# Token layout p\*16+i with whole transfers, full-array transforms, a second product path and a new instruction order in an S4-plus-gated-MLP kernel

## The chip, the cores and the metric

The kernel runs on 1 core of one Trainium2 chip. The metric is the device time of one execution in microseconds (us), lower is better. A profile gives the span from the first to the last instruction, which is about 2 us shorter than that time (276.0 of 278.0 us before). Engines are PE (TensorE, matmuls), DVE (VectorE), ACT (ScalarE), POOL (GpSimd) and SP (which only issues transfers here). Each has its own list of instructions, in the order in which the program emits them; semaphores join the lists. PSUM is the memory that PE writes its results to here, in banks; the other tiles are in SBUF.

## The reference, cut to what matters

```python
x  = A_u                                  # (1, 2048 tokens, 512)
xn = layernorm(x)
# branch A: S4 convolution. A kernel K (512 x 2048) is made from 128 complex modes,
#   K = real(einsum("dn,dnl,dn->dl", C, exp(dt*A*l), dt*B)),
# then y = irfft(rfft(xn, 4096) * rfft(K, 4096))[:2048] + xn * Dskip
# branch B: gated MLP, F = 1792
h  = sigmoid(xn @ w_gate) * (xn @ w_up)
out = x + A(xn) + h @ w_down
```

## The kernel before

Everything is a plan: each operation is added with its engine and dependencies, and a literal list `ORDER` of operation numbers says in which order they are emitted. The per-engine program is that list, filtered by engine. So `ORDER` decides, for each engine, what stands in front of what.

```python
ORDER = [1, 29, 0, 3, 2, 39, 12, 14, ... ]       # 930 numbers, found off-line
...
    def run(self):
        for n in ORDER or range(len(self.ops)):
            op = self.ops[n]
            for s in op.acq:                      # takes a buffer (a PSUM bank, an SBUF slot)
                s.idx = self.free[s.pool].pop(0)
            for s in op.rel:
                self.free[s.pool].append(s.idx)
            yield op
```

The gated part, four groups of 512 tokens with 14 slices each. There are only three PSUM banks ("gu") for gate and up results:

```python
def fg(...):                                       # gate: 4 matmuls 128x128x512
    T.matmul(bank(sl)[:, c0:c1], w[:, kt, k * 128:(k + 1) * 128], xnT[:, grp, kt, c0:c1], ...)
S.activation(out=hT_sb[...], in_=bank(a), func=ACT.Sigmoid)            # ACT frees the gate bank
def fu(...):                                       # up: 4 matmuls
    T.matmul(bank(sl), wu_sb[:, kt, k * 128:(k + 1) * 128], xnT[:, grp, kt, :], ...)
def fpd(sl=b, h=h):                                # DVE reads the up result out of PSUM
    V.tensor_tensor(out=h(), in0=h(), in1=bank(sl), op=ALU.mult)
prods.append(pl.add("DVE", 0.60, fpd, [es_, mu], PPROD, rel=[b]))      # and frees its bank
```

The convolution: a first transform (matrix S1), four blocks of correlation matmuls that build K from tables which DVE multiplies up (`cmul`), and for each of 16 units a second transform, products with the transform of K, an inverse transform, a trip through DRAM (`z_scr`, `v_scr`), and a last transform (S2).

```python
xv = A_u[0].rearrange("(a j i) d -> j a i d", j=2, i=NT)     # token a*32+j*16+i on partition 64*j+a
# load, store and sum: two transfers of 64 partitions each
for j in range(2):                                           # first transform: two half arrays
    T.matmul(bank(sl, j), s1[64 * j:64 * j + 64, :], xn[64 * j:64 * j + 64, i, :], ...)
for j in range(2):                                           # last transform: two half arrays
    T.matmul(o[64 * j:64 * j + 64, DW * p:DW * p + DW], s2[:], vps[p][t][:, j, r, :], ...)
```

## Time and profile before

| | before |
|---|---|
| time, median | 275.44 us (275.18 to 279.31, 4 runs) |
| span of the profiled run | 276.0 us (this execution took 278.01 us, more than the median) |
| mean granted clock (TensorE, 1 is full speed), same run | 0.965 |
| busy PE, DVE, ACT, same run | 229.2, 208.6, 162.7 us |

No engine is full over the whole run, so stages have to be looked at. I cut the trace at five events: the first gated matmul, the ends of the first, second and last block of correlation matmuls, and the end of the last inverse transform. The windows view of the kernel before, columns named in the first line here (busy us of each engine, number of instructions in brackets, granted clock, DMA share, GB/s):

```profile
core 0: us, PE busy (x) PEld busy (x) DVE busy (x) ACT busy (x) POOL busy (x), PEclk, DMA share, GB/s
0.00:15.17 15.17, 8.32 (x38) 4.27 (x39) 7.66 (x23) 5.01 (x9) 4.25 (x14) 0.86 0.72 190
15.17:94.60 79.43, 70.39 (x438) 31.51 (x437) 74.59 (x152) 72.01 (x117) 8.15 (x14) 0.96 0.59 158
94.60:121.20 26.60, 24.47 (x303) 12.08 (x302) 25.86 (x58) 13.13 (x23) 1.98 (x4) 1.00 0.55 146
121.20:195.70 74.50, 59.22 (x865) 33.48 (x865) 66.73 (x125) 41.37 (x62) 3.17 (x7) 0.98 0.49 136
195.70:242.80 47.10, 40.77 (x471) 23.33 (x471) 17.77 (x24) 28.36 (x35) 3.27 (x4) 0.96 0.70 184
242.80:276.00 33.20, 26.04 (x180) 12.96 (x179) 15.97 (x28) 2.81 (x4) 0.00 (x0) 0.97 0.55 162
```

Up to 195.7 us DVE is nearly full: in the second to fourth row it is busy 74.59 + 25.86 + 66.73 = 167.2 of 180.5 us. Behind that point PE has the most work. The gated products in the groups view (busy us, mean ns of one, idle before):

```profile
L964 DVE TENSOR_TENSOR hT_sb<-hT_sb,bank 128x512 bf16<-128x512 bf16 x56 | 37.0, 682 | 10.7 <-PE bank L957 6.0 <-ACT hT_sb L951 3.7 <-ACT ln_m_f L467 0.8
```

A product is recorded with 0.682 us and holds DVE 0.60 us when products follow one another (two of them take DVE from 35.46 to 36.66 us). Three lines of the chain of waits (start, us, what) show the start: the transposes wait for the identity matrix, and the first gated matmuls follow at 15.4 us.

```profile
4.63 7.99 DMA ident<-c_ident
12.66 1.87 PE pair L522 x16
...
15.38 12.50 PE bank L942 x64
```

### The profile page before, as it was taken

What the parts mean: (1) busy time and instruction counts of PE and PEld (TensorE: products, weight loads), DVE (VectorE), ACT (ScalarE), POOL (GpSimd) and SP (SyncE); (2) the same over time, 40 slices, a digit from 0 to 9 for tenths busy, and PEclk for the clock granted to TensorE, in tenths of its full rate; (3) what the DMA queues carried; (4) which work ended last, traced back from release to release, by engine and by line L of the source; (5) the groups of instructions that cost most, each with busy time, mean ns of one, the idle gap of its engine ahead of it and who ended that gap; (6) DMA issues with size and microseconds to landing.
All of it is one profiled execution on the core that took longest, in us unless ns stands there. A gap on an engine that the chain in (4) does not pass through costs nothing.

```text
span 276.0 us, 5805 instructions
## 1 busy us (share of the span) xinstructions
PE 229.2 (83%) x2290; PEld 117.6 (43%) x2290; DVE 208.6 (76%) x407; ACT 162.7 (59%) x249; POOL 20.8 (8%) x43
## 2 busy tenths in 40 slices
PE   7299997969969899878598878596998689799792
PEld 2264433323323544355354445243665345444441
DVE  3579899998999999999979997979153222685172
ACT  2289999998998572558385549341356758531000
POOL 3225000020020002003000000000011200000000
PEclk9779999997999999999999999989999979999998
DMA  5899992122066764451765751454386984665743
GB/s 152 190 297 306 201 307 77 40 57 76 31 190 160 233 160 128 100 183 28 184 185 143 222 159 46 130 153 125 93 221 178 223 199 112 190 187 181 217 134 97
DMA packets 51069, 43.42 MB, mean 157 GB/s; under 512 B 13153, under 2 KB 44258, under 8 KB 51042
## 3 DMA queue, kind: packets, MB, share of 16 engines
q1 hardware_dynamic: 47506, 38.73, 50.1%
q0 software_dynamic: 960, 1.57, 3.9%
q10 hardware_dynamic: 2576, 2.75, 3.5%
q8 instruction: 18, 0.29, 0.5%
q14 instruction: 9, 0.07, 0.1%
HBM read 24.43 MB, written 12.06 MB: 132 GB/s over the span
## 4 chain that ended last, share of the span: by engine, by line
PE 40%; DVE 29%; DMA 16%; ACT 6%; issue 4%; SPq 2%; DVEq 0%; ACTq 0%
PE bank L942 11%; PE bank L957 9%; DMA big<-z_scr 8%; PE bank L982 6%; DVE big L681 5%; DVE big L680 5%; PE pair L744 4%; DVE hT_sb L964 4%; PE pair L835 4%; DVE big L685 4%; DVE big L686 3%; DMA ident<-c_ident 3%; DMA big<-big 2%; DMA big<-v_scr 2%; SPq L397 2%
## 5 line engine op out<-in xcount | busy, mean ns | idle before, releaser
L942 PE MATMUL bank<-xnT,wg_sb 128*128 128x512 bf16 (+1 forms) x236 | 57.4, 382 | 1.4 <-ACT hT_sb L951 1.4
L957 PE MATMUL bank<-xnT,wu_sb 128*128 128x512 bf16 x224 | 55.9, 384 | 2.9 <-ACT hT_sb L951 1.5
L982 PE MATMUL bank<-wd_sb,hT_sb 128*128 128x512 bf16 x224 | 52.2, 387 | 3.3 <-ACT glu_sb L1012 3.3
L964 DVE TENSOR_TENSOR hT_sb<-hT_sb,bank 128x512 bf16<-128x512 bf16 x56 | 37.0, 682 | 10.7 <-PE bank L957 6.0
L951 ACT ACTIVATE hT_sb<-bank 128x512 bf16<-128x512 f32 x56 | 32.3, 599 | 15.1 <-PE bank L942 15.0
L841 DVE TENSOR_TENSOR big<-big 128x2048 bf16<-128x2048 bf16 x16 | 19.6, 1223 | 24.8 <-DMA big<-big 8.2
L680 DVE TENSOR_TENSOR big<-big 128x256 bf16<-128x256 bf16 (+5 forms) x52 | 33.1, 636 | 2.5 <-ACT big L721 1.4
L942 PEld LDWEIGHTS <-wg_sb 128*128 128x128 bf16 x236 | 22.8, 101 | 27.9 <-issue 6.8
L982 PEld LDWEIGHTS <-hT_sb 128*128 128x128 bf16 x224 | 21.7, 99 | 30.4 <-issue 6.9
L681 DVE TENSOR_TENSOR big<-big 128x256 bf16<-128x256 bf16 (+5 forms) x52 | 32.9, 633 | 0.0
L957 PEld LDWEIGHTS <-wu_sb 128*128 128x128 bf16 x224 | 20.5, 98 | 28.5 <-issue 7.7
L822 ACT ACTIVATE big<-pair 128x1024 bf16<-128x1024 f32 x16 | 16.3, 1026 | 11.4 <-PE pair L817 7.3
L685 DVE TENSOR_TENSOR big<-big 128x128 bf16<-128x128 bf16 (+5 forms) x52 | 21.9, 420 | 0.8
L835 PE MATMUL pair<-big 128*128 128x256 bf16 x160 | 20.4, 278 | 2.2 <-ACT big L837 0.7
L862 ACT ACTIVATE big<-pair 128x1024 bf16<-128x1024 f32 x16 | 16.4, 1026 | 9.0 <-PE pair L858 5.2
L686 DVE TENSOR_TENSOR big<-big 128x128 bf16<-128x128 bf16 (+5 forms) x52 | 21.6, 416 | 0.0
L837 ACT ACTIVATE big<-pair 128x1024 bf16<-128x1024 f32 x16 | 16.4, 1027 | 7.8 <-PE pair L835 3.4
L835 PEld LDWEIGHTS <-big 128*128 128x128 bf16 x160 | 15.9, 100 | 8.2 <-issue 3.0
L744 PE MATMUL pair<-big 128*32 128x82 bf16 x512 | 11.5, 257 | 8.2 <-DVE big L685 6.3
L645 ACT ACTIVATE big<-pair 128x1024 bf16<-128x1024 f32 x16 | 16.3, 1019 | 1.7 <-DMA z_scr<-big 1.0
L858 PE MATMUL pair<-big 64*64 64x256 bf16 x384 | 13.7, 272 | 3.1 <-ACT big L822 1.6
L817 PE MATMUL pair<-big,m 64*64 64x256 bf16 x128 | 6.6, 288 | 10.2 <-DMA big<-z_scr 10.2
(84 smaller groups left out, 234.2 us busy)
## 6 DMA issues: line engine op xcount, KB each, us to landing
big<-c_E SPq DMA_DIRECT2D x16, 320.0 KB, 4.2
z_scr<-big SPq DMA_DIRECT2D x16, 256.0 KB, 2.6
big<-z_scr SPq DMA_DIRECT2D x16, 256.0 KB, 4.6
big<-big SPq DMA_DIRECT2D x64, 64.0 KB, 2.9
v_scr<-big SPq DMA_DIRECT2D x16, 256.0 KB, 2.6
big<-v_scr SPq DMA_DIRECT2D x12, 256.0 KB, 4.6
big<-in_A_u_dram SPq DMA_DIRECT2D x8, 256.0 KB, 7.2
wu_sb<-in_B_w_up_dram SPq DMA_DIRECT2D x2, 896.0 KB, 6.1
```

What stands on the lines that cost most here:

```text
L680: V.tensor_tensor(out=wide(outp), in0=lov, in1=mre, op=ALU.mult)
L681: V.tensor_tensor(out=wide(tb()), in0=lov, in1=mim, op=ALU.mult)
L685: V.tensor_tensor(out=outp[:, :, :, 0, :], in0=outp[:, :, :, 0, :], in1=tb()[:, :, :, 1, :], op=opr)
L686: V.tensor_tensor(out=outp[:, :, :, 1, :], in0=outp[:, :, :, 1, :], in1=tb()[:, :, :, 0, :], op=opi)
L744: T.matmul(pk[32 * t:32 * t + 32, y % 4, :], G[:, r, :, comp, h], H[:, r, :, comp, h], start=(comp == 0), stop=(comp == 1), tile_position= ...
L835: T.matmul(two(sk)[:, o:o + DW], es()[:, g, kt, :], kT[p][:, kt, :], start=kt in (0, NKT - 1), stop=kt >= NKT - 2)
L841: V.tensor_tensor(out=pp().rearrange("p q h m -> p (q h) m"), in0=xx().rearrange("p q h m -> p (q h) m"), in1=kb()[:, 0:2 * DW].unsqueeze( ...
L942: T.matmul(bank(sl)[:, c0:c1], w[:, kt, k * 128:(k + 1) * 128], xnT[:, grp, kt, c0:c1], start=(kt == 0), stop=(kt == KT - 1))
L951: S.activation(out=hT_sb[:, hs.idx, k % 2, :], in_=bank(sl), func=ACT.Sigmoid)
L957: T.matmul(bank(sl), wu_sb[:, kt, k * 128:(k + 1) * 128], xnT[:, grp, kt, :], start=(kt == 0), stop=(kt == KT - 1))
L964: V.tensor_tensor(out=h(), in0=h(), in1=bank(sl), op=ALU.mult)
L982: T.matmul(bank(po), hT_sb[:, hts[k // 2].idx, k % 2, jj * 128:(jj + 1) * 128], wd_sb[:, k, :], start=(k == 0), stop=k == FT - 1, **kw)
```

## The change

The intent by its description: lay tokens on partitions as p\*16+i, so that each load, sum and store is one plain transfer over 128 partitions, and pad the first and last transform with zeros to the full array. The diff does two more things: 32 of the 56 second factors are copied out of PSUM by ACT to bf16 in SBUF (I call this an eviction), from where the DVE product is shorter (0.68 us from PSUM, 0.42 us for a bf16 product of the same size in SBUF, in the trace of before); and `ORDER` is a new list, found with other cost figures. Those figures are used by the off-line search only; nothing in the running kernel reads them.

```diff
+UEV = (5, 7, 11, 14, 16, 18, 21, 22, 24, 25, ... 48, 53)          # 32 of 56
 ORDER = [
-    1, 29, 0, 3, 2, 39, ...                                       # 930 numbers
+    ...                                                           # 964 numbers, all new
-    return 16e3 * pkt / (pkt / 27.0 + 21.0)                       # planner only
+    pkt = min(pkt, 2048)
+    return 16e3 * pkt / (pkt / 26.5 + 8.5)
-    xv = A_u[0].rearrange("(a j i) d -> j a i d", j=2, i=NT)
+    xv = A_u[0].rearrange("(p i) d -> p i d", i=NT)
-    ls = [load("ACT" if i0 < 4 and j else "SP", xn[64 * j:64 * j + 64, i0:i0 + n, :], xv[j][:, i0:i0 + n, :], ...) for j in range(2)]
+    ls = [load("ACT" if i0 == 2 else "SP", xn[:, i0:i0 + n, :], xv[:, i0:i0 + n, :], ...)]
-    T.matmul(bank(sl, j), s1[64 * j:64 * j + 64, :], xn[64 * j:64 * j + 64, i, :], start=True, stop=True)
+    T.matmul(bank(sl, j), s1[:, j, :], xn[:, i, :], start=True, stop=True)
-    T.matmul(o[64 * j:64 * j + 64, DW * p:DW * p + DW], s2[:], vps[p][t][:, j, r, :], start=start, **kw)
+    T.matmul(o[:, DW * p:DW * p + DW], s2[:, j, :], vps[p][t][:, j, r, :], start=start and j == 0, **kw)
-    mm = pl.add("PE", 0.85, f_k, ...)                             # planner's cost of a correlation half
+    mm = pl.add("PE", 1.30, f_k, ...)
+    def feu(sl=b, us=us, on=on):
+        if on:
+            S.activation(out=us_sb[:, us.idx, :], in_=bank(sl), func=ACT.Identity)
+    eu = pl.add("ACT", 0.48, feu, [mu], PSIG, acq=[us] if on else [], rel=[b] if on else [], ...)
-    V.tensor_tensor(out=h(), in0=h(), in1=bank(sl), op=ALU.mult)
+    V.tensor_tensor(out=h(), in0=h(), in1=us_sb[:, us.idx, :] if on else bank(sl), op=ALU.mult)
# cut: stores, sums and corrections in the same manner; E stored contiguously; other planner costs
```

## The prediction

> **What bounds the kernel now.** No single engine. The page's busy totals are PE 229, DVE 209, ACT 163 of 276 us, but stretch by stage: 20 to 57 us everything is full (PE 34.7, DVE 35.3, ACT 36.5 of 37); 57 to 90 us DVE 31.7 and ACT 30.3 of 33; 90 to 196 us DVE 97.2 of 106, PE 87.8, ACT only 56.4; from 196 us DVE is light (33.7 of 80) and PE (66.5) waits for DMA hops. The chain of waits agrees: mostly DVE from 33 to 124 us, then PE mixed with DMA (8% of the span is the reload of z_scr). The first 15 us are lost to PE: its transposes wait 4.1 us for the identity, which is issued seventh on its queue and takes 8.0 us.
>
> **What the change does.**
> 1. 32 of the 56 products of the gated part get their second factor through ScalarE as bf16 in SBUF. Today such a product (PSUM operand) holds DVE 0.60 us (0.68 recorded); a bf16 SBUF product of 128x512 in the same trace takes 0.34 (0.42 recorded). [...] DVE loses 32 x 0.26 = 8.3 us; ACT gains 32 x 0.50 = 16 us. 28 of the 32 come before the last convolution block (196 us), 23 of them after the first gated group and most of a second, where ACT is half idle. That is the real gain.
> 2. First transform: two 64-row matmuls side by side become two full-array ones. Pure work 0.22 to 0.43 us, but today each lone pair costs about 0.41 us[...] (start-to-start of its neighbours at 70.6 to 71.0 us). [...] So nearly free.
> 3. Last transform: 8 half-width matmuls take about 0.50 us now; full width, 0.86. Six of them: +2.2 us of PE, late, partly in waits. Corrections double in number but stay narrow: about +0.5 us.
> 4. Transfers of 2 x 64 partitions become one of 128: about 18 fewer issues, 0.5 to 0.6 us each on SP and ACT queues; in the tail the eight stores per queue from 263 to 273 us shrink.
> 5. The instruction order is new: identity is first, so PE may start its gated matmuls 2 to 3 us earlier; but the first gate weights are issued later and x comes third.
> 6. E is stored contiguously; 4.2 us to landing now, perhaps a little less.
>
> **Sum.** DVE's saving before 196 us is 28 x 0.26 = 7.3 us. In the early stages ACT is full, so I count 4.5; PE at over 90% stops more. Start -1.5; tail: stores -1, transforms +1.5; reordering and steadier DMA -1. Predicted **269.0 us**, 8 in 10 within **263.5 to 275.0**. Chances: faster by over 2% 0.60, within 2% 0.37, slower 0.03.
>
> **What would show it.** By-form groups: 24 products at 680 ns and 32 at about 420; 32 more ACT evictions near 0.6 us; first transforms 128x128 with no idle before. Windows: DVE busy near 200 us; ACT near 179; PE near 233. The last correlation matmuls (195.7 us now) should end near 189 to 191. The stretch after them stays about 80 us. PE's first gated matmul comes before 14 us.
>
> **What would make it wrong.** ACT, full until 57 us, takes the extra evictions on the critical path; PE becomes the limit in 90 to 196 us; a single-queue load of x delays the start; in the last 80 us, DMA hops (store v, reload v, final transforms) are less covered, because the new order leaves only two down projections after the last inverse transform: this could return 3 us. The opposite: better hiding there gives more.

The sum: 275.4 - 4.5 - 1.5 - 1 + 1.5 - 1 = 268.9 us, given as 269.0. That the first transforms are nearly free enters it as 0.

## More of the kernel before

The page of the kernel before, totals per engine and then the granted TensorE clock in 40 equal slices of 6.9 us (tenths of full speed, 9 is 90% or more):

```profile
PE 229.2 (83%) x2290; PEld 117.6 (43%) x2290; DVE 208.6 (76%) x407; ACT 162.7 (59%) x249; POOL 20.8 (8%) x43
...
PEclk9779999997999999999999999989999979999998
```

## The result, and the profile after

The time after is 257.05 us (256.20 to 257.33, 4 runs) against 275.44: 18.4 us less. The ratio is 0.933, with a 95% interval of 0.930 to 0.936. Ratios here are the mean time of one kernel's fast runs over that of the other's of the same rounds, so not quite the ratio of the medians. The prediction said 269.0, with 263.5 to 275.0: the direction was right, the size was outside the range.

The page of the kernel after, totals and granted clock (40 slices of 6.4 us):

```profile
PE 224.0 (88%) x2274; PEld 120.9 (48%) x2306; DVE 199.7 (78%) x407; ACT 174.2 (68%) x279; POOL 16.5 (6%) x37
...
PEclk9999999999999999889999999999999999999998
```

The windows view of the kernel after, cut at the same five events:

```profile
0.00:12.95 12.95, 4.47 (x22) 2.51 (x23) 8.09 (x22) 6.31 (x11) 4.54 (x14) 1.00 0.84 227
12.95:88.60 75.65, 74.00 (x461) 35.64 (x468) 73.67 (x158) 73.86 (x126) 6.52 (x12) 1.00 0.54 158
88.60:110.00 21.40, 18.46 (x266) 9.71 (x268) 20.53 (x48) 12.27 (x23) 2.10 (x4) 0.92 0.85 223
110.00:177.80 67.80, 61.36 (x887) 35.15 (x896) 64.99 (x130) 50.38 (x79) 0.71 (x4) 1.00 0.49 134
177.80:226.50 48.70, 43.56 (x493) 25.91 (x500) 21.37 (x35) 30.40 (x40) 2.62 (x3) 1.00 0.77 211
226.50:254.40 27.90, 22.18 (x157) 12.03 (x158) 11.05 (x18) 1.02 (x1) 0.00 (x0) 0.97 0.53 163
```

The groups view of the kernel after, products and evictions:

```profile
L978 ACT ACTIVATE us_sb<-bank 128x512 bf16<-128x512 f32 x32 | 19.3, 606 | 5.1 <-DVE hT_sb L982 5.0
L982 DVE TENSOR_TENSOR hT_sb<-hT_sb,bank 128x512 bf16<-128x512 bf16 x24 | 16.0, 681 | 5.3 <-ACT big L832 4.7 <-PE bank L967 0.5
L982 DVE TENSOR_TENSOR hT_sb<-hT_sb,us_sb 128x512 bf16<-128x512 bf16 x32 | 13.1, 415 | 2.1 <-ACT hT_sb L961 2.1
```

Where the 21.6 us between the two spans went (3.2 us more than between the medians, because the profiled execution of before took 278.0 and that of after 256.2 us):

| stage | before | after | difference |
|---|---|---|---|
| start, to the first gated matmul | 15.2 | 13.0 | -2.2 |
| to the end of the last correlation block (three rows) | 180.5 | 164.9 | -15.6 |
| to the last inverse transform | 47.1 | 48.7 | +1.6 |
| tail | 33.2 | 27.9 | -5.3 |

In the long middle stage DVE's busy time fell from 167.2 to 73.67 + 20.53 + 64.99 = 159.2 us (-8.0), about what the 28 evictions up to there save by themselves (28 x (0.682 - 0.415) = 7.5 us). But its idle time fell as well, from 13.3 to 164.9 - 159.2 = 5.7 us (-7.6), and no part of the diff saves that by making an instruction shorter. TensorE's mean granted clock rose from 0.965 to 0.990.

Four theories fit this. Layout: whole transfers and plain transforms remove waits. Evictions: a lighter DVE lets everything behind it flow. Order: the new list is better by itself, and possibly the only one in which evictions pay. Clock: PE ran slower in the trace of before, and DVE waited for it.

### The profile page after: what moved, and what is told of

Its sections match the earlier page's. It is cut to its first block, busy times and chain, and to the rows that moved or that the text cites. A ratio compares the mean times of both kernels' runs of the same rounds, so it can differ in the third digit from the quotient of the medians.

```text
span 254.4 us, 5790 instructions
## 1 busy us (share of the span) xinstructions
PE 224.0 (88%) x2274; PEld 120.9 (48%) x2306; DVE 199.7 (78%) x407; ACT 174.2 (68%) x279; POOL 16.5 (6%) x37
## 4 chain that ended last, share of the span: by engine, by line
DVE 45%; PE 26%; DMA 14%; SPq 7%; issue 3%; ACT 2%; DVEq 0%; ACTq 0%
DVE big L690 10%; DVE big L691 9%; DMA big<-z_scr 7%; SPq L407 7%; PE bank L952 7%; DVE big L695 6%; PE bank L967 6%; DVE big L696 5%; DVE hT_sb L982 5%; DVE big L851 3%; DMA big<-v_scr 3%; DMA v_scr<-big 3%; PE bank L495 2%; PE bank L1000 2%; PE pair L845 2%
## 5 line engine op out<-in xcount | busy, mean ns | idle before, releaser
L952 PE MATMUL bank<-xnT,wg_sb 128*128 128x512 bf16 (+1 forms) x226 | 54.9, 370 | 1.1 <-issue 0.3
L967 PE MATMUL bank<-xnT,wu_sb 128*128 128x512 bf16 x212 | 53.0, 379 | 1.0 <-issue 0.5
L1000 PE MATMUL bank<-wd_sb,hT_sb 128*128 128x512 bf16 x216 | 50.4, 379 | 0.7 <-issue 0.2
L1000 PEld LDWEIGHTS <-hT_sb 128*128 128x128 bf16 x224 | 21.6, 98 | 25.6 <-issue 1.1
L978 ACT ACTIVATE us_sb<-bank 128x512 bf16<-128x512 f32 x32 | 19.3, 606 | 5.1 <-DVE hT_sb L982 5.0
L845 PE MATMUL pair<-big 128*128 128x256 bf16 x160 | 19.8, 273 | 0.8 <-DVE big L789 0.8
L982 DVE TENSOR_TENSOR hT_sb<-hT_sb,bank 128x512 bf16<-128x512 bf16 x24 | 16.0, 681 | 5.3 <-ACT big L832 4.7
L653 PE MATMUL pair<-big,s 128*128 128x512 bf16 x30 | 9.3, 394 | 8.9 <-DVE big L521 8.2
L731 ACT ACTIVATE big<-big 128x256 bf16<-128x256 bf16 x32 | 13.3, 446 | 2.3 <-PE pair L754 2.3
```

The costliest lines, as they stand in the source:

```text
L845: T.matmul(two(sk)[:, o:o + DW], es()[:, g, kt, :], kT[p][:, kt, :], start=kt in (0, NKT - 1), stop=kt >= NKT - 2)
L978: S.activation(out=us_sb[:, us.idx, :], in_=bank(sl), func=ACT.Identity)
L982: V.tensor_tensor(out=h(), in0=h(), in1=us_sb[:, us.idx, :] if on else bank(sl), op=ALU.mult)
L1000: T.matmul(bank(po), hT_sb[:, hts[k // 2].idx, k % 2, jj * 128:(jj + 1) * 128], wd_sb[:, k, :], start=(k == 0), stop=k == FT - 1, **kw)
```

## The experiments

To move one part alone, I gave each operation a name in both plans (for example "up matmul of group 2, slice 5") and translated either order list to either kernel. Where an operation is two half transfers in one and one transfer in the other, the halves stand next to each other. All 18 runs gave correct results. The chips differ. The state of a run matters as well: a run over 1.5% above the fastest of its kernel counts as slow, the others as fast, and ratios use fast runs alone; e12 shows what lies behind it.

### e1: the layout alone, in the old order

```diff
 # the kernel after, but
-UEV = (5, 7, 11, ...)
+UEV = ()
-ORDER = [... list of after ...]
+ORDER = [... list of before, by name ...]
```

> The change's token layout, whole transfers, full-array transforms and contiguous E, but the old instruction order and no product through ScalarE. If the plain transfers carry the gain: 265 us or less. If the order or the ScalarE evictions carry it: 273 to 277 us, with the last correlation matmuls near 194 us as in the kernel before.

275.02 us against 277.88 (ratio 0.990, interval 0.981 to 0.9998). In its trace the first gated matmul starts at 11.6 us and the last correlation block ends at 191.0 instead of 195.7 us, but the tail is 34.8 us long. So the layout alone is worth about 1%, and the theory that it carries the gain falls for the old order.

### e2 and e3: the evictions in the old order, with and without the layout

```diff
 # e2: as e1, with the evictions. e3: the kernel before, plus
+    eu = pl.add("ACT", 0.48, feu, [mu], PSIG, acq=[us] if on else [], rel=[b] if on else [])
-    prods.append(pl.add("DVE", 0.60, fpd, [es_, mu], PPROD, rel=[b]))
+    prods.append(pl.add("DVE", 0.33, fpd, [es_, eu, mu], PPROD, rel=[us] if on else [b]))
 # both: in ORDER, each eviction stands just before its product
```

> As e1, and the 32 second factors go through ScalarE, each eviction placed just before its product in the old order. If the lighter VectorE is the cause by itself: 265 us or less, VectorE busy near 200 us. If the new order is needed to use it: 268 to 274 us, because ScalarE, full until 57 us, meets the extra work in the wrong places.

> The kernel before with only the 32 evictions added, old order, old layout. Expected within 2 us of e2 if the layout is nearly neutral; 4 us or more slower than e2 if the plain transfers matter.

e2: 290.78 us (ratio 1.042). e3: 292.96 us (ratio 1.054, interval 1.045 to 1.063). Neither answer stated for e2 was right: they ended at 274 us. e3 lies 2.2 us above e2, between its two answers. Both kernels are 13 to 15 us slower than before. DVE is busy only 201.2 us in e3, so the saving in work is there. The groups view of e3 shows where it is lost:

```profile
L979 DVE TENSOR_TENSOR hT_sb<-hT_sb,us_sb 128x512 bf16<-128x512 bf16 x32 | 13.4, 423 | 32.1 <-ACT us_sb L975 31.9
```

32 fast products take 13.4 us, and DVE stands idle 32.1 us in front of them, 31.9 of it waiting for the eviction on ACT.

### e4: the evictions and the new order, with the old layout

```diff
 # e3, but
-ORDER = [... list of before, by name ...]
+ORDER = [... list of after, by name ...]
```

> The kernel before with the evictions and the new order, but the old layout: half transfers side by side, half-array transforms. If order and evictions make the gain: 257 to 261 us. If the layout carries it: 266 us or more.

258.47 us against 277.88 (ratio 0.929, interval 0.920 to 0.937). The whole gain is there without the layout.

### e5: the new order with most evictions undone

```diff
 # the kernel after, but
-UEV = (5, 7, 11, ... 48, 53)                     # 32
+UEV = (18, 28, 30, 33, 45, 48, 53)               # 7; without these the bank pool runs empty
 # in ORDER, the other 25 products move forward to the place of their eviction or sigmoid
```

> The kernel after, with 25 of its 32 evictions undone (the other 7 can't be without a deadlock on banks): each such product reads PSUM again and stands where its eviction or its sigmoid stood, whichever is later. VectorE gets about 6.5 us back. If the new order carries the gain without the evictions: 258 to 263 us. If order and evictions need each other: 265 to 275 us.

264.49 us, two of its four runs slow; its fast runs took 261.05 and 263.96 against 278.27 to 282.12 of before (ratio of the fast runs 0.935). So the new order, with the layout and 7 evictions, holds most of the gain without the other 25. That is a little above what I wrote for the order alone, and below what I wrote for the case in which both need each other.

### e6: an attempt to slow the products down

```diff
-    us_sb = const.tile([128, 2, 512], BF, name="us_sb")
+    us_sb = const.tile([128, 2, 514], BF, name="us_sb")       # and use [:, us.idx, 1:513]
```

> The kernel after, unchanged in order and evictions, but the evicted factor starts at an odd element of its row, so that the 32 products may lose their fast rate (0.42 us recorded) and take about 0.68 again. If they do and VectorE bounds the kernel up to the last correlation matmuls: 7 to 8 us more, 264 to 266 us. If VectorE is not the bound there: under 260 us. If the products stay at 0.42 us the run says nothing.

256.79 us. The groups view of e6 says why this tells nothing about DVE: the products kept their rate, 418 ns each with a factor that starts at an odd element, against 415 in the trace of after. That such a start might slow them was my guess, and the run does not show it.

```profile
L982 DVE TENSOR_TENSOR hT_sb<-hT_sb,us_sb 128x512 bf16<-128x512 bf16 x32 | 13.2, 418 | 3.3 <-ACT hT_sb L961 3.3
```

A miss as an experiment. It serves as a copy of the kernel after beside e5: the 25 evictions are worth the difference of their fast runs, 262.5 against 256.9 us (means), 5.6 us. Their traces, both at a clock of 0.98, show where: from the first gated matmul to the last correlation block DVE is busy 164.0 us in e5 and 158.8 in e6, and this stretch takes 169.6 and 164.4 us. Work taken off DVE comes off the time there almost one for one.

### e7 and e8: evictions in the old order, placed early

```diff
 # e3, but each eviction stands in ORDER right after its up matmul (later if both us slots are taken)
-UEV = (5, 7, 11, ...)
+UEV = (28, 29, ... 43)                            # e7 only: 16 products where ACT is half idle
```

> The kernel before, old order and layout, with 16 evictions only, of the products from 90 to 196 us where ScalarE is half idle, each issued right after its up matmul. If the lighter VectorE alone is worth its 16 x 0.26 us: 271 to 273 us. If an eviction in an order that was not made for it costs more in waits than it saves: 275 us or more.

> As e3, all 32 evictions in the old order, but each right after its up matmul instead of just before its product. If e3 lost its time by the late placement: 270 to 276 us. If it lost it to the full ScalarE of the first 90 us: 283 us or more.

e7: 280.62 us against 280.99 (ratio 0.997, interval 0.988 to 1.005), no gain. (The stated limits were set for a kernel before at 275 us; on this chip it takes 281, so the ratio decides.) e8: 298.3 us (ratio of the fast runs 1.054), not better than e3, so the late placement was not the fault. In its trace the first correlation block ends at 103.2 instead of 94.6 us and the last at 209.8 instead of 195.7: more than half of the loss falls into the first stage, where ACT was fullest before (72.0 of 79.4 us), the rest later. In that trace ACT stands idle 23.9 us directly in front of the evictions, waiting for their up matmuls: placed early, they hold up ACT. (Its clock was 0.931, lower than the 0.965 of before, so not all of the loss need come from the evictions.) e7 is the sharpest test of my prediction, because I had counted on exactly these products. Its group of fast products:

```profile
L979 DVE TENSOR_TENSOR hT_sb<-hT_sb,us_sb 128x512 bf16<-128x512 bf16 x16 | 6.5, 419 | 7.1 <-ACT us_sb L975 7.1
```

The saving of 16 x 0.26 = 4.2 us is more than paid back by 7.1 us of DVE waiting for ACT. In all, DVE idles 19.9 us between the first gated matmul and the last correlation block, against 13.3 before. Two waits of 3.4 us make up most of the 7.1. In one, at 158 us, the eviction stands on ACT behind an instruction that waited 2.9 us for a transfer (store of `v_scr`). In the other, at 185 us, ACT itself was idle for 3.3 us because the up matmul came late. So ACT had time, but not at that place of the order, or not with its input ready.

### e9 to e11: the order alone, and its two parts

```diff
 # e9: the kernel before (old layout) with the ORDER and the 7 evictions of e5
 # e10: list of before up to the last correlation matmuls, then list of e9 (11 operations
 #      put off until a bank was free), 3 evictions left
 # e11: list of e9 up to the last correlation matmuls, then list of before (4 put off), 6 left
```

> The kernel before with nothing but the new order (old layout; 25 of the 32 evictions undone as in e5, 7 left). If the order by itself carries most of the gain: 262 to 266 us, a ratio of 0.93 to 0.955. If it needs the layout or the evictions: 269 us or more.

> The kernel before in the old order up to the last correlation matmuls (195.7 us in its trace), then in the new order. The two stages behind that point took 80.3 us before and 76.6 after, so 3 to 4 us less (ratio 0.985 to 0.99) if the new order's tail works by itself; no change or slower if the tail only fits what the new order leaves for it.

> The mirror of e10: new order up to the last correlation matmuls, old order behind. If the order's gain lies in the first part (VectorE without gaps): last correlation matmuls near 183 us, total 264 to 268 us (ratio 0.955 to 0.97). If it lies in the tail: above 272 us.

e9: 264.28 us (264.12 to 264.47). e10: 276.56 (274.01 to 278.02). e11: 266.52 (266.48 to 268.74), its last correlation matmuls ending at 185.1 us. The kernel before took 273.03 to 283.24 on that chip, median 280.89, and only its 273.03 (clock 0.987) counts as a fast run. I therefore compare with that run alone: the order is worth 273.0 - 264.3 = 8.7 us, and its first part alone 6.5 us. One run is a thin base, but e12 below, the old order with its clock kept up, took 272.3 us, which makes it 8.0. Against the median of before it is 16.6 us, because that kernel's usual clock is lower. For the new tail behind the old first part no gain is shown: e10 is 3.5 us above the one fast run, but at a lower clock (0.962 to 0.980), and inside the range of before. The windows view of e9 at the same events as above, second to fourth row:

```profile
13.99:92.90 78.91, 74.51 (x468) 33.44 (x467) 76.63 (x158) 69.38 (x115) 7.35 (x13) 1.00 0.53 158
92.90:114.70 21.80, 18.50 (x269) 9.48 (x268) 21.04 (x49) 11.79 (x22) 3.62 (x6) 0.97 0.82 216
114.70:185.20 70.50, 63.48 (x897) 35.19 (x896) 67.43 (x129) 44.23 (x67) 0.72 (x4) 0.99 0.46 129
```

DVE is busy 165.1 of 171.2 us: 6.1 us idle against 13.3 before. The gap is closed by the order, without the layout and with four evictions in this stretch. The same stretch in the other traces agrees: DVE idles 10.9 us in e1, 14.1 in e10 and 12.5 in e12, which have the old order there, and 5.5 to 8.0 us in e4, e5, e6, e9, e11, e13 and e14, which have the new one.

### e12: the old order, with TensorE kept busy in four gaps

Why does one and the same kernel take 273 us once and 283 us another time? Over the 43 executions of the kernel before, the granted clock lies between 0.932 and 0.987 and the time between 284.7 and 273.0 us, with a correlation of -0.82. In the traces of before and after the clock is either full or half. The halved stretches last 3.4 or 6.8 us, and the last one of each runs past the end of the trace. Each of the five others begins inside a gap of 2.2 to 4.1 us in PE's work or 1.0 us behind one. Not every such gap has one: those of before of 2.8 us up to 135.6 us and of 2.6 us up to 192.8 us have none. In the trace of before one runs from 11.0 to 17.8 us. It begins inside the 4.1 us in which PE waits for the identity and goes on over the first gated matmuls, as two rows of the windows view show (the clock stands before the last two columns):

```profile
10.00:14.00 4.00, 1.34 (x13) 1.34 (x13) 2.33 (x7) 1.68 (x5) 0.00 (x0) 0.62 0.72 170
14.00:18.00 4.00, 4.00 (x22) 2.69 (x21) 3.34 (x10) 2.96 (x4) 1.46 (x3) 0.52 1.03 323
```

From the mean clock, (1 - 0.965) x 276.0 / 0.5 = 19 us of that execution ran at half clock, and (1 - 0.990) x 254.4 / 0.5 = 5 us of the one after.

```diff
 # the kernel before, plus 62 matmuls into a free bank, result never read
+    for n, pool in ((6, "po"), (18, "po"), (11, "gu"), (12, "po"), (15, "gu")):
+        more_warm(n, pool)       # before the first transform and the first transposes, before the last down projection
+                                 # of the first group, before the second transforms of units 1.1 and 1.5
```

> The kernel before with 62 matmuls of no use put into four gaps of its TensorE (before the first transposes, before the last down projection of the first group, before two of the later transforms), to test whether its half-clock stretches (17 us in its trace, against 3.4 us in the trace of after, the last stretch of both left out) carry the gain. If they do: 266 to 271 us. If the matmuls under half clock were not on the critical path: 273 to 277 us with a granted clock above 0.98.

272.29 us (271.10 to 273.43, 4 runs), against 273.0 to 283.2 of before: about as fast as that kernel's best execution, each time. The stated limits, 266 to 271 for one answer and 273 to 277 for the other, leave 272.3 between them. Its clock in 40 slices:

```profile
PEclk9999999999999999999779999997999999999998
```

The start now keeps its clock, and the halved stretches near 62 and 223 us are gone; one from 132 to 139 us comes instead, and one near 183 us stays. So halved clock is a real cost of the old order and goes with most of its scatter, but it can't explain 257: with the best clock the old order stays above 271 us. Nor does it explain DVE's gaps. The windows view of e12 at the same events, second to fourth row:

```profile
14.62:92.00 77.38, 70.49 (x448) 31.32 (x448) 73.63 (x150) 72.29 (x117) 8.16 (x14) 1.00 0.59 158
92.00:118.70 26.70, 24.56 (x307) 12.15 (x304) 25.98 (x58) 13.11 (x23) 1.99 (x4) 1.00 0.58 152
118.70:193.30 74.60, 64.11 (x877) 34.91 (x878) 66.55 (x125) 41.18 (x62) 3.18 (x7) 0.93 0.50 135
```

DVE is busy 166.2 of 178.7 us: with full clock in the first two rows it still idles 12.5 us in all.

### e13 to e16: layout once more, and two attempts to go further

```diff
 # e13: the kernel after. e14: e4 again. e15: the kernel after, but in ORDER
-    ..., ld x2 (ACT), ln_m2, o_dt, ld wg0 (ACT), ...
+    ..., ld x2 (ACT), ld wg0 (ACT), ln_m2, o_dt, ...
 # e16: e15, plus 9 matmuls of no use before the second correlation block
```

> The kernel after, unchanged, to stand on the same chip as e14 to e16: 256 to 258 us.

> e4 once more, beside e13. If layout, whole transfers and full-array transforms are nearly neutral under the new order: within 2 us of e13. If they carry a part of the gain: 3 us or more slower than e13.

> The kernel after, with the load of the first gate weights issued second on the ScalarE queue instead of behind a ScalarE operation that waits for another load (TensorE waited 0.8 us for these weights). If the start is on the path to the end: 0.5 to 1.5 us less than e13. If VectorE, saturated behind, takes it back: within 0.3 us.

> e15 with 9 matmuls of no use in the 2.2 us gap before the second block of correlation matmuls, after which the clock was halved for 3.4 us. If that stretch costs: 0.3 to 1 us less than e15; a granted clock above 0.985. If not: the same as e15.

e13: 257.36 us. e14: 257.53 us. Ratios 0.928 and 0.929 against before. Under the new order the layout is worth nothing that six runs each can show.

e15: 259.71 us, slower than e13 by 2.3 us (medians; the fast runs take 257.63 to 260.06 and 255.69 to 258.96), against both answers that I had written. The DMA view of e13, then of e15 (size, median us from issue to landing):

```profile
wg_sb<-in_B_w_gate_dram ACTq DMA_DIRECT2D x1, 384.0 KB, 7.8
...
big<-in_A_u_dram SPq DMA_DIRECT2D x1, 256.0 KB, 4.0
```

```profile
wg_sb<-in_B_w_gate_dram ACTq DMA_DIRECT2D x1, 384.0 KB, 5.9
...
big<-in_A_u_dram SPq DMA_DIRECT2D x1, 256.0 KB, 6.2
```

The weights, issued 4.5 us earlier, are now in flight together with the second load of tokens of x (issued at 1.2 and 1.6 us), whose landing time goes from 4.0 to 6.2 us. The layernorm waits for the tokens, and the first gated matmul moves from 13.4 to 14.9 us. The load that looked late was out of the way.

e16: 257.62 us (257.27 to 258.04), 2.1 us under e15 and with a granted clock of 0.996 to 1.0 in all six runs, but no better than e13. Its first gated matmul is as late as in e15 (14.7 us), so how much of a late start reaches the end stays open.

### e17 and e18: the nine matmuls alone

```diff
 # e17: the kernel after, plus
+    warm = pl.add("PE", 0.2155 * 9, lambda: [T.matmul(bank(warm.tab), ident[:], xnT[:, 0, 0, :], start=True, stop=True)
+                                             for _ in range(9)], tab=_Slot("po"))   # before the second correlation block
 # e18: the kernel after
```

> The kernel after with only the nine matmuls of e16 before the second block of correlation matmuls. e16 was 2 us under e15; if that was the clock, this is 1 to 2.5 us under e18 and its granted clock is 0.995 or more in every run. If it was chance: within 0.5 us of e18.

> The kernel after, unchanged, beside e17: 255.5 to 258.5 us, slower where the granted clock is lower.

e17: 257.45 us (255.55 to 259.71). e18: 258.73 us (255.75 to 259.91). The ranges lie over each other, and the clock of e17 was 0.984 to 1.0, not 0.995 or more throughout. Inconclusive: no version here is shown to beat the kernel after.

## Why the prediction was right or wrong

**The sum, as measured.** At a like clock (0.98 to 0.99), before takes 273.0 us (its one fast run in the call of e9), the order alone 264.3 (e9), order and evictions 257.5 (e14), and the layout on top 257.4 (e13). The order gives about 8.7 us and the evictions within it about 6.8; the layout nothing visible. e9 and e14 come from different chips and e9 still holds 7 evictions, so the split is good to perhaps 2 us (e5 against e6, on one chip, gives 5.6 for 25 evictions). The rest of the 18.4 us, about 2.4, is that before took 275.4 in the first measurement and not 273.0. A lower clock would fit (-0.82 over the 43 executions above), but the clocks of those four executions are not on record (the profiled one, 278.0 us, had 0.965), nor is their chip, so it is not shown.

**What bounds the kernel: it fits.** DVE up to the last correlation block, as e5 against e6 shows for the new order; PE and transfers behind, by the busy times only. After the change that block ends at 177.8 us, far below the 189 to 191 that I had stated, and in the second window PE and ACT are as full as DVE (74.00, 73.86 and 73.67 of 75.65 us).

**"Reordering and steadier DMA -1": wrong, and this is the step that failed.** I treated the new list as a small bonus of 1 us. With only 7 evictions left and the old layout it is worth 8 to 9 us at a like clock (e9), nearly half of the gain: DVE idles 6.1 instead of 13.3 us between the first gated matmul and the last correlation block. I had the number 13.3 in reach, since the windows of before show it, but I costed only instructions that became shorter and not the gaps that another order can close.

**"That is the real gain" of the evictions: half right.** The costs were right: 32 products at 415 ns and 24 at 681, evictions of 606 ns, DVE 199.7 us in all. I counted 4.5 us for them and they gave about 6.8. But they give it only in an order made for them. In the old order all 32 cost 15 us (e3) and 16 in the half-idle stretch gain nothing (e7), since DVE then waits 31.9 and 7.1 us for the evictions.

**"ACT, full until 57 us, takes the extra evictions on the critical path": did not happen** in the new order. ACT is fuller than before in the second window (73.86 of 75.65 us against 72.01 of 79.43), and the window still became 3.8 us shorter.

**First transforms "nearly free": right.** Layout and padding together are neutral (e13, e14), though SP and ACT issue 16 transfers fewer (186 against 202). "No idle before" was wrong: PE idles 8.9 us in front of the first transforms, 8.2 of it until the layernorm is done. What rests on the traces is the spacing: a lone pair of half-array matmuls took about 0.41 us in the trace of before (70.6 to 71.0 us), a pair of full ones takes 0.43 us in that of after (14.33 to 14.76 us). Why the half-array pair took that long was not shown.

**The start, -1.5: about right** (-2.2 in the traces, first gated matmul at 12.95 us, "before 14"). **The tail, +0.5: wrong.** From the last correlation block on it is 80.3 to 76.6 us, and I had expected a loss there from fewer down projections as cover. e10 shows no gain of the new tail behind the old first part; e11 against e9 (266.5 to 264.3) that it is worth some 2 us behind the new one.

**Busy times: one right, one near, one wrong.** DVE 199.7 (near 200). ACT 174.2, where I said 179: ACT loads its activation tables three times instead of five, 1.28 us each, in e9 too, so that comes from the order; it is 2.6 of the 4.8 us. PE 224.0 instead of 233: some matmul records are missing (2274 matmuls against 2306 weight loads), but the trace of e13 has all 2306 and shows 225.9 us, so they make up some 2 us. The rest fits fewer matmuls at half clock, which I left out (e5, with as many, shows 229.8 us at 0.981, e13 at 0.997). **"E ... perhaps a little less": wrong,** 4.9 us to landing instead of 4.2; no run shows whether that cost anything.

**What stays open.** Which of the many moves inside the new list closes DVE's gaps was not isolated. That it was found with truer costs is plausible: the planner's 0.85 us for half a correlation block became 1.30, and the trace of before shows about 1.4 for such a half. But no run tests the planner.

## What to carry to other kernels

When a diff carries a re-planned instruction order, cost the idle time of the bounding engine as well as its work: the gaps are what a new order can take, and here they were worth as much as the shortened instructions. Moving work to an engine with spare time paid here only in an order made for it; look at the wait in front of the consumer, not at the busy share of the helper. And before comparing two kernels, look at the granted clock of each run: here one execution of before ran 19 us at half clock, in stretches that mostly begin in gaps of TensorE's work, and with four of its gaps filled the kernel took 272.3 us (e12) where before took 273.0 to 283.2.
